# GpSimd issues three more transfers of an inverse transform, with a new order of work behind its last stage

## The chip, the cores and the metric

The kernel runs on one core of one Trainium2 chip. The metric is the device time of one execution in microseconds. Engines are named as the profile names them: PE (TensorE, matmuls), PEld (its weight loads), DVE (VectorE), ACT (ScalarE), POOL (GpSimd) and SP (SyncE, which only issues transfers). Transfers (DMAs) are issued from SP, ACT or POOL, and 16 DMA engines move the data.

## The reference

One layer on x of shape (2048 positions, 448 channels): a gated long convolution, then an MLP that mixes the positions. Cut to what matters:

```python
k_shift = sum_t k_pad[:, t:t+S, :] * shift_k[:, 3-t]         # short causal filter, 4 taps
kv = k_shift * v
y = irfft(rfft(kv, 2S) * rfft(ssm_k, 2S))[:S] + kv * ssm_D   # long convolution, per channel
h = x + layernorm(x) * y                                      # layernorm over the 448 channels
n = layernorm(h)
u = gelu(einsum("sd,sf->df", n, w1) + b1)                     # contracts the 2048 positions
out = h + (einsum("df,fs->ds", u, w2) + b2).T
```

All inputs are bfloat16; S = 2048, D = 448, F = 1792.

## The kernel before

Position s is split as s = 16 q + r, so a tile of row r has the 128 values of q on the partitions and the 448 channels in the free dimension. The transform of the convolution is done with matmuls in two stages. Between the stages data changes partitions, and that is done with SBUF-to-SBUF transfers.

**Forward stages.** k1 and u1 (first stages of the filter and of kv), k2 and u2 (second stages, `emit_stage2`, L1095 the matmuls).

**First inverse stage, i1** (`emit_products_i1`, L1151). It runs over eight pairs jj; pair jj holds the columns j = 2jj and 2jj + 1. For each half h (real and imaginary part) DVE forms products of the two spectra (L1161), PE multiplies by a constant table (L1178, 8 matmuls), and an evacuation copies the two PSUM banks to the tile TU (`evac`, L739 on ACT, L742 on DVE). Then transfers carry TU to TZ, the input of the second inverse stage, where the row r stands in the free dimension. For all pairs but the last, each column has two transfers (L1201): a large one of 112 partitions (196 KB), which fills rows 0 to 13 of TZ, and a small one of 16 partitions (28 KB), which fills rows 14 and 15. The large ones go over POOL, except for j = 3, which goes over SP; the small ones go over SP. The last pair, jj = 7, has four transfers of 98 KB instead (L1190), one for each column and half, which fill rows 2 to 15: three over SP and one over ACT. Rows 0 and 1 do not wait for them, since they take that pair's part from TU by extra matmuls (L1308).

**Second inverse stage, i2** (`emit_i2`, L1284). For each of the 16 rows r, PE does two matmuls with the transposed table ET (L1300; 4 more, L1308, for r = 0 and 1). Then a *gate* for r >= 4 (L1317 on ACT or L1319 on DVE: times the inverse deviation of x, plus 1), a *comb* on DVE (L1337 for r < 4, reading PSUM and the normalized x, called XN; L1327 otherwise), the statistics of h (L1343 and L1346 for r = 0 and 1; a square on ACT, L1355, and small POOL instructions L1365 to L1375 for the others), a power on POOL (L1379) and on DVE the normalized row Q (L1386).

**Beside it.** `emit_q` takes the statistics of x (DVE L1237 and L1239, POOL L1245 and L1248), `emit_xn` makes XN for r < 4 (POOL L1257, DVE L1260, ACT L1270), `emit_ct` transposes the table to ET in three late groups ct.0 to ct.2 (PE L1109, evacuated by ACT, L739), and `emit_warm` has 14 dummy matmuls (L1211) whose result is not used.

**MLP.** Seven column groups of the first product accumulate over the rows in seven of the eight PSUM banks (L1433), row by row as Q arrives, with the i2 matmuls of the later rows between them. Then come the other seven groups (L1443), the gelu (L1423) and the second product (L1455), whose rows are written out. The weights are loaded over SP: four loads of W1A (L1406), four of W1B (L1410) and four of W2 (L1417). All W1A loads but the first wait until the last pair's transfers have landed.

**What sets the order.** The table `ORDER` at the head of the file holds, for each engine, the list of its operations; each engine works through its list in order. An entry `step:n` or `step:a-b` names operations of a step. A planner (`schedule`, L323) walks through these lists only to place PSUM banks and to find which semaphore waits are needed; all waits come from data dependences. The entries that matter here:

- i1.1, i1.4, i1.6, i1.8, i1.10, i1.12, i1.14, i1.16 are the pairs jj = 0, 1, 2, 3, 4, 5, 6, 7. PE does them in the order 0, 6, 3, 4, 5, 2, 1, 7, so i1.4 (jj = 1) and i1.16 (jj = 7) are the last two.
- In such a step operations 9 and 18 are the evacuations of h = 0 and h = 1, and 19, 20, 21, 22 are the transfers: large and small of the even column, large and small of the odd one. In i1.4 the numbers are one lower (18 large of j = 2, 19 small of j = 2, 20 large of j = 3, 21 small of j = 3). In i1.16, 19 and 20 are the transfers of h = 0, and 21 and 22 those of h = 1.
- i2.1 and i2.2 are the matmuls of r = 0 and i2.3 its comb, i2.8 its Q; i2.9 and i2.10, i2.11, i2.16 the same of r = 1; i2.18 and i2.21 the combs of r = 2 and 3, i2.39 and i2.52 the Q of r = 4 and 6. q.n are statistics of x (q.2 for r = 2 and 3, q.3 and q.4 for r = 4 to 7, q.5 and q.6 for 8 to 11, q.7 and q.8 for 12 to 15), xn.n the steps of XN, mlp.r:n the matmuls of row r of the first product.

## Time and profile before

| what | value |
|---|---|
| runs | 173.05 us median of 3 (173.01 to 173.22) |
| profiled execution | 173.14 us, span 171.3 us, granted PE clock 1.000 |
| busy, share of the span | PE 94%, PEld 55%, DVE 59%, ACT 54%, POOL 34% |
| DMA | 35.15 MB, mean 205 GB/s |
| chain that ended last | PE 66%, ACT 17%, DMA 7%, DVE 5%, POOL 2% |
| first L1300 (i2) matmul | 75.27 us from the span's start |
| first L1433 (MLP) matmul | 81.08 us |

Times of day in the text are microseconds from the start of the span. A line of the chain of work that ended last gives start, length and what ran or was waited for. A line of the timeline gives start, length, engine, line, operation, tiles and, in brackets, how long the engine idled before and what released it; a q behind an engine's name means its sequencer, which issues transfers. A line of the waits gives who waited for whom, total, number of times and the longest. The data of most of the kernel lies in one tile called arena, and PSUM is called ps. The PE busy share counts pipelined matmuls, so it is read together with the chain.

### The profile page before, as it was taken

The numbers are of one execution on the slowest core, as the hardware profiler recorded it, in microseconds if no ns is written. First come the engines' busy times: TensorE is split into PE (matmuls) and PEld (weight loads), VectorE is DVE, ScalarE is ACT, GpSimd is POOL, SyncE is SP. The second block draws the span as 40 slices with busy tenths as digits, with TensorE's granted clock in tenths as the row PEclk, the third lists the DMA queues.
The fourth block names the chain that finished last, engine by engine and source line by source line (L and its number), as shares of the span: only waits on it lengthen the run. The fifth ranks groups of instructions, "written<-read, shape, count | busy, mean of one in ns | idle before, by whom it ended". The sixth has DMA issues, their size and how long they took to land.

```text
span 171.3 us, 3572 instructions
## 1 busy us (share of the span) xinstructions
PE 161.9 (94%) x1425; PEld 94.9 (55%) x1425; DVE 101.4 (59%) x188; ACT 92.6 (54%) x132; POOL 59.0 (34%) x151
## 2 busy tenths in 40 slices
PE   6999999789889999968999999999999999999994
PEld 2785755342334333544455555555567777777783
DVE  7998988859999999979989830000003123132231
ACT  3699698978999999979866537321210000000000
POOL 8346637571810686245897830000000000000000
PEclk9999999999999999999999999999999999999999
DMA  5999678593859757646899999990000111101111
GB/s 163 420 352 354 210 234 311 178 354 136 286 144 369 268 167 208 176 143 214 266 331 384 411 420 419 415 406 33 0 0 4 54 54 54 54 0 57 54 54 54
DMA packets 15652, 35.15 MB, mean 205 GB/s; under 512 B 3692, under 2 KB 9804, under 8 KB 15636
## 3 DMA queue, kind: packets, MB, share of 16 engines
q1 hardware_dynamic: 12588, 28.45, 45.6%
q0 software_dynamic: 2784, 6.29, 11.5%
q8 instruction: 11, 0.18, 0.4%
q10 hardware_dynamic: 264, 0.18, 0.3%
q14 instruction: 5, 0.04, 0.1%
HBM read 22.05 MB, written 1.84 MB: 139 GB/s over the span
## 4 chain that ended last, share of the span: by engine, by line
PE 66%; ACT 17%; DMA 7%; DVE 5%; POOL 2%; issue 1%; SPq 0%; DVEq 0%
PE ps L1455 25%; PE ps L1433 12%; PE ps L1443 12%; ACT arena L739 9%; DMA arena<-arena 7%; ACT arena L1070 4%; PE ps L1178 4%; PE ps L1095 3%; ACT arena L848 2%; PE ps L1026 2%; PE ps L1300 2%; POOL arena L1076 2%; PE ps L993 2%; DVE arena L1008 2%; PE ps L1060 1%; DVE arena L1337 1%
## 5 line engine op out<-in xcount | busy, mean ns | idle before, releaser
L1458 DVE SCALAR_TENSOR_TENSOR arena<-ps,arena 128x448 bf16<-128x448 f32 (+2 forms) x17 | 11.1, 656 | 56.9 <-PE ps L1455 56.9
L1455 PE MATMUL ps<-arena 128*128 128x448 bf16 (+2 forms) x238 | 42.7, 342 | 0.0
L1455 PEld LDWEIGHTS ps<-arena 128*128 128x128 bf16 x238 | 33.3, 145 | 9.5
L739 ACT CAST arena<-ps 128x896 bf16<-128x896 f32 x30 | 24.6, 1016 | 0.2 <-PE ps L1095 0.2
L1433 PE MATMUL ps<-arena 128*128 128x448 bf16 x112 | 22.5, 353 | 0.7 <-DVE arena L1375 0.7
L1070 ACT CAST arena<-ps 128x896 bf16<-128x896 f32 x24 | 20.5, 918 | 3.0 <-PE ps L1060 2.9
L1076 POOL DMA_DIRECT2D arena<-arena x32 | 17.5, 553 | 12.5 <-ACT arena L1070 10.4
L1443 PE MATMUL ps<-arena 128*128 128x448 bf16 x112 | 21.4, 352 | 0.0
L1423 ACT ACTIVATE arena<-ps,arena 128x448 bf16<-128x448 f32 x14 | 8.3, 634 | 18.9 <-PE ps L1443 14.7
L1095 PE MATMUL ps<-arena 128*64 128x448 bf16 x128 | 15.2, 359 | 2.6 <-DMA arena<-arena 1.0
L1433 PEld LDWEIGHTS ps<-arena 128*128 128x128 bf16 x112 | 10.8, 98 | 11.3 <-DVE arena L1375 1.1
L1161 DVE TENSOR_TENSOR arena<-arena 128x1792 bf16<-128x1792 bf16 x16 | 16.7, 1086 | 0.3 <-ACT arena L739 0.2
L1443 PEld LDWEIGHTS ps<-arena 128*128 128x128 bf16 x112 | 11.0, 98 | 10.2
L1060 PE MATMUL ps<-arena 128*32 128x448 bf16 x256 | 15.2, 355 | 0.8 <-DVE arena L1008 0.5
L1178 PE MATMUL ps<-arena 64*128 64x448 bf16 x128 | 14.5, 351 | 0.1
L1201 POOL DMA_DIRECT2D arena<-arena x13 | 7.7, 597 | 13.7 <-ACT arena L739 13.7
L1095 PEld LDWEIGHTS ps<-arena 128*64 128x64 f16 x128 | 5.8, 108 | 11.0 <-ACT arena L739 2.9
L1178 PEld LDWEIGHTS ps<-arena 64*128 64x128 f16 x128 | 6.1, 94 | 8.2 <-ACT arena L739 2.5
L1008 DVE TENSOR_TENSOR arena<-ps,arena 128x512 bf16<-128x512 f32 (+1 forms) x16 | 9.1, 619 | 2.1 <-PE ps L993 1.8
L739 ACT COPY arena<-ps 128x1024 bf16<-128x1024 bf16 (+1 forms) x8 | 7.8, 1022 | 4.5 <-PE ps L967 3.4
L1355 ACT ACTIVATE arena<-arena 128x448 bf16<-128x448 f32 x14 | 8.0, 573 | 4.0 <-DVE arena L1327 3.8
L1060 PEld LDWEIGHTS ps<-arena 128*32 128x32 f16 x256 | 5.1, 95 | 7.8 <-DVE arena L1008 2.5
(96 smaller groups left out, 195.1 us busy)
## 6 DMA issues: line engine op xcount, KB each, us to landing
arena<-in_B_w_dram SPq DMA_DIRECT2D x8, 896.0 KB, 6.5
arena<-in_B_w_dram SPq DMA_DIRECT2D x2, 2048.0 KB, 17.0
arena<-arena POOLq DMA_DIRECT2D x32, 112.0 KB, 3.3
arena<-arena SPq DMA_DIRECT2D x16, 224.0 KB, 3.2
arena<-in_B_w_dram SPq DMA_DIRECT2D x2, 1536.0 KB, 19.3
arena<-arena POOLq DMA_DIRECT2D x13, 196.0 KB, 4.3
arena<-in_A_k_dram SPq DMA_DIRECT2D x4, 448.0 KB, 5.3
arena<-in_A_v_dram SPq DMA_DIRECT2D x4, 448.0 KB, 8.4
```

The costliest lines, as they stand in the source:

```text
L739: return e.copy(out=dst(), in_=src())
L1008: return e.tensor_tensor(out=v, in0=u.rearrange("p t (r d) -> p t r d", d=64), in1=v, op=ALU.mult)
L1060: op("pe", lambda e, W, b=b, r=r, q=q, x=x, c0=c0: e.matmul(PS[32 * q:32 * q + 32, b.slots[x], 0:D], E[:, 2 * r + x, c0:c0 + 32], src[:, r ...
L1070: return e.copy(out=dst, in_=Ppair(b)) if W == "act" else e.tensor_copy(out=dst, in_=Ppair(b))
L1076: shuf[tag].append(op(q_, lambda e, W, g=g, i=i, a=a, nu=nu, jh=jh: e.dma_start(T[a + i:a + i + 4 * nu - 3:4].rearrange("p (j k) c d -> p ...
L1095: op("pe", lambda e, W, b=bs[h], h=h, j=j, c=c, par=par: e.matmul(PS[64 * par:64 * par + 64, b.slots[c], 0:D], FW[:, 64 * c:64 * c + 64], ...
L1161: op("dve", lambda e, W, m=m, i=i: e.tensor_tensor(out=MR(m.slots[0]).rearrange("p (x y) d -> p x y d", x=2), in0=TU[:, i].unsqueeze(2).br ...
L1178: k = op("pe", lambda e, W, b=bs[h], m=ms[h], par=par, t=t, tab=tab, xy=xy, P=P: e.matmul(Pb(b, par), tab[P, :], MR(m.slots[0])[P, xy, :], ...
L1433: op("pe", lambda e, W, r=r, fc=fc, b=bs[fc]: e.matmul(Pb(b), W1A[:, r, 128 * fc:128 * fc + 128], Q[:, r, :], start=(r == 0), stop=(r == R ...
L1443: op("pe", lambda e, W, r=r, fc=fc, b=b: e.matmul(Pb(b), W1B[:, r, 128 * (fc - n0):128 * (fc - n0) + 128], Q[:, r, :], start=(r == 0), sto ...
L1455: op("pe", lambda e, W, r=r, fc=fc, b=b, d0=d0, d1=d1: e.matmul(Pb(b)[:, d0:d1], W2[fc // 7][:, fc % 7, r:S:R], G[:, fc, d0:d1], start=(fc ...
L1458: op("dve", lambda e, W, r=r, b=b, A=A, d0=d0, d1=d1: e.scalar_tensor_tensor(out=X[:, r, d0:d1], in0=Pb(b)[:, d0:d1], scalar=bm[:, r:r + 1 ...
```

## The change

Three transfers change their issuer. The small transfers of the pair jj = 2 (i1.6:20 and i1.6:22) go from SP to POOL. One of the last pair's four (i1.16:21, h = 1 of column 14) goes from ACT to POOL.

```diff
-k = op("act" if h and par == 0 else "sp", lambda e, W, j=j, h=h, p0=p0: e.dma_start(
+k = op("pool" if h and par == 0 else "sp", lambda e, W, j=j, h=h, p0=p0: e.dma_start(
...
-for q_, a, b_, j0 in (("sp" if j == 3 else "pool", 0, 112, 0), ("sp", 112, 128, 14)):
+for q_, a, b_, j0 in (("sp" if j == 3 else "pool", 0, 112, 0), ("pool" if jj == 2 else "sp", 112, 128, 14)):
```

The lists in `ORDER` change from about the last two pairs of i1 on. On SP ten of the small transfers, which stood behind the last pair's and between the W1A loads, now stand ahead of i1.4:20, and two (i1.4:21 and :19) stand directly behind it; the W1A and W1B loads follow each other. On PE three more dummy matmuls stand ahead of i1.16, the table transposes come in another order, three dummies stand between the i2 matmuls, and the rows and the MLP's column groups come in another order. On DVE one small instruction of the statistics goes behind the first comb, and the combs of r = 2 and 3 go ahead of the statistics of r = 1. On ACT the gates of r = 4 to 6 go behind the squares of r = 2 and 3.

```diff
 PE
-warm.9 warm.11 warm.5 warm.8 warm.1 i1.16:1-7 i1.16:10-16 i1.16:8 i1.16:17 warm.10 warm.4 warm.7 warm.6 warm.0
-ct.2:0-7 warm.12 warm.3 ct.0:0-7 ct.1:0-6 warm.2 i2.1:0-1 i2.2:0-3 i2.9:0 ct.1:7 i2.9:1 i2.10:0-3 i2.28 i2.17
-i2.45 i2.20 i2.41 i2.32 i2.54 mlp.0:6 mlp.0:1 mlp.0:5 mlp.0:2-4 mlp.0:0 i2.58 mlp.1:6
+warm.9 warm.11 warm.5 warm.8 warm.1 warm.10 warm.0 warm.4 i1.16:1-7 i1.16:10-17 i1.16:8 ct.0:0-7 warm.2 ct.1:0-2
+warm.6 ct.2:0-6 ct.1:3-7 i2.1:0-1 i2.2:0-3 ct.2:7 i2.9:0-1 warm.7 i2.10:0-3 i2.17 i2.45 i2.20 i2.32 warm.3
+warm.12 i2.41 i2.28 i2.54 mlp.0:4 mlp.0:2 mlp.0:1 mlp.0:5 mlp.0:0 mlp.0:6 i2.58 mlp.0:3 mlp.1:4
 ACT
-i1.16:18 i1.16:9 i1.16:21 ct.2:8 ct.0:8 xn.4 ct.1:8 xn.5 i2.29 i2.46 i2.19 i2.33 i2.22 i2.42 i2.31
+i1.16:18 i1.16:9 ct.0:8 xn.4 ct.1:8 ct.2:8 xn.5 i2.46 i2.19 i2.22 i2.29 i2.42 i2.33 i2.31
 DVE
-q.4:0 q.4:2-3 q.4:1 q.3:1-3 q.5:0 q.5:2-3 q.5:1 q.6:2 q.6:0-1 q.7:0 q.7:2 xn.3:1 i2.3 q.6:3 i2.4 i2.11 i2.5
-i2.12 i2.6 i2.18 i2.21 q.7:3 i2.13 i2.8 i2.14 i2.55 i2.30 i2.16 q.7:1
+q.3:1-2 q.4:0 q.3:3 q.4:2 q.5:0 q.5:2 q.5:1 q.4:3 q.4:1 xn.3:1 q.5:3 q.6:2 q.6:0 q.7:2 q.7:0 i2.3 q.6:1 q.6:3 i2.4
+i2.11 i2.5 i2.18 i2.6 i2.21 i2.12 i2.13 i2.8 i2.14 i2.55 i2.30 i2.16
 POOL
-i1.6:19 i1.6:21 i1.4:18 q.4:4-5 q.2:4-5 xn.3:0 q.6:4-5 ... i2.49:1-2 q.8:4 i2.50 q.8:5 i2.51
+i1.6:19 i1.6:21 i1.6:20 q.2:4 i1.4:18 i1.6:22 q.2:5 xn.3:0 i1.16:21 q.4:4-5 q.6:4-5 ... i2.49:1-2 q.8:4-5 i2.50 i2.51
 SP
-i1.6:22 i1.1:20 i1.1:22 i1.4:20 i1.16:22 i1.16:20 i1.16:19 w1a.1 i1.12:22 i1.14:20 i1.4:21 i1.4:19 w1a.2 i1.6:20
-i1.14:22 i1.10:20 i1.10:22 w1a.3 i1.8:22 i1.12:20 i1.8:20 w1b
+i1.14:20 i1.1:20 i1.1:22 i1.12:22 i1.10:22 i1.10:20 i1.12:20 i1.8:20 i1.8:22 i1.14:22 i1.4:20-21 i1.4:19
+i1.16:22 i1.16:20 i1.16:19 w1a.1 w1a.2 w1a.3 w1b
```

66 rows, old and new, of the table ORDER are left out of this document.

## The prediction

> **What bounds the kernel now.** I read the page's chain first, then the chain in order of time, then the waits, then the issues around the place where the chain leaves the engines. The chain, cut to the stretch that the change touches and to what follows:
>
> ```profile
> 69.06 1.13 ACT arena L739
> 70.20 0.28 issue
> 70.48 4.74 DMA arena<-arena
> 75.22 0.05 issue
> 75.27 0.55 PE ps L1300 x2
> 75.82 0.77 PE ps L1308 x4
> 76.59 0.02 issue
> 76.62 0.68 DVE arena L1337
> ...
> 80.63 0.40 DVE arena L1386
> 81.02 0.07 DVE arena L1375
> 81.10 1.48 PE ps L1433 x7
> ...
> 105.16 21.19 PE ps L1443 x112
> 126.34 42.08 PE ps L1455 x231
> ```
>
> Columns are start, length and what (us). From 81.08 (first L1433) to 168.42 the chain is PE alone, back to back, and the change adds and drops no matmul there. So the time is the start of the first L1433 matmul plus a constant, unless PE stalls later. Before it stand one transfer of 4.74, 1.3 of PE work for row r = 0, and a DVE chain of 4.4 that ends with Q of r = 0 (L1386). The waits (total, times, longest) say the same:
>
> ```profile
> PE ps L1300 <- DMA arena<-arena: 1.3, 1, 1.3
> DVE arena L1337 <- PE ps L1308: 0.9, 1, 0.9
> PE ps L1433 <- DVE arena L1375: 0.7, 1, 0.7
> ```
>
> The transfer is i1.4:18, the last large one of GpSimd. Around it the issues are:
>
> ```profile
> 66.97 3.92 SPq L1201 DMA_DIRECT2D arena<-arena  x4
> 67.24 1.17 POOL L1201 DMA_DIRECT2D arena<-arena  x2 [1.48 <-ACT arena L739]
> 70.48 0.59 POOL L1201 DMA_DIRECT2D arena<-arena  x1 [2.08 <-ACT arena L739]
> 72.26 2.19 SPq L1190 DMA_DIRECT2D arena<-arena  x3
> ```
>
> The fourth of SP's is i1.4:20, the other large half of the same pair, issued at 70.21. The answer on line L1201 gives the landings of GpSimd's transfers:
>
> ```profile
> DMA to landing us min/median/max: 3.0/4.3/5.4
> ```
>
> Why does i1.4:18 take 4.74 and not 3.0? I added up the trace's DMA packet records (of 500 bytes and more) in quarter microseconds. When GpSimd alone moves one transfer, 8.0 packets are in flight (58.25, 63.25, 64.50); where two of its successive transfers overlap there are 13 to 14 (66.00, 67.50). So one uses 8 of 16 engines and the next the other 8. But from 72.25 to 74.25 GpSimd's and SP's packets sum to 8 again (1.0+7.6, 4.1+4.0, 6.1+1.8, 6.1+2.0, 6.9+1.2, 6.0+2.2, 4.9+3.2, 2.9+5.5): i1.4:18 and i1.4:20 share one set of 8 while the other lies idle. The first data packet of i1.4:18 leaves 1.94 after its issue, against 1.17 for i1.14:19. They land at 75.22 and 75.06.
>
> **The change, part by part.** Times are of the profiled execution: 173.14, its span 171.3 and 1.8 around it; the three runs have a median of 173.05, 0.09 lower.
>
> *The small transfers on GpSimd.* i1.6:20 goes in at 68.41, right behind i1.6:21, into the 2.08 that POOL idles there (0.59 by the L1201 rows), and q.2:4 (0.2 to 0.5) after it still ends before 70.2: i1.4:18 is issued at 70.48 as before. It is one more transfer in GpSimd's sequence, so i1.4:18, until now the 13th, becomes the 14th and takes the other set. Alone there it should need what i1.14:19 and i1.10:19 needed alone (2.98 and 2.97): landing 73.46; i1.6:21, ahead of it on that set, had all but one packet moved by 72.0, so I take 73.5 to 74.0. The ends of this cost are no gain (75.22, still shared) and 73.46; I take the lower since the packet sums are its nearest row. The Trainium skill, page "DMA: Bandwidth & Descriptors", section "Why a DMA increments its semaphore by 16 and not by 1", says that a transfer from SP takes the lowest-numbered engines, and one of GpSimd's the next ones behind a round-robin cursor; the trace agrees (the sums of 8 and 13 to 14), but no run here shows the cursor moved by a small transfer. i1.4:20 has its set to itself: first packet 71.54 as before, 130 KB/us as it moved in 71.5 to 72.5, 200 KB: 73.1, landed 73.3.
>
> *i1.6:22 and i1.16:21 on GpSimd.* i1.6:22 costs POOL 0.59 from 71.07 (idle before: 1.04). q.2:5 and xn.3:0 (0.71 and 0.19) follow and end at 72.7, nearly 2 earlier than before. i1.16:21 waits for the evacuation i1.16:18 and holds back q.4:4-5 (0.24 + 1.05), which ends at 75.0 and not 73.5; its readers are the gates of r = 4 to 7 on ACT, first at 77.4. ACT loses an issue of 1.51, which left it idle 0.78; the L739 work behind it then waits for PE anyway (0.37 idle before ct.1:8), so I count 0.
>
> *SP.* Eleven transfers of 28 KB leave the stretch 77.56 to 86.33 behind the last pair: ten go to earlier places on SP, one (i1.6:20) to POOL, and i1.6:22 leaves 66.97. Each costs SP 0.67. i1.14:20, i1.1:20 and i1.1:22 fit at 60.1 to 62.1, where SP idles; i1.12:22 waits for its evacuation (ACT ends it at 63.71) and with six more takes 7 x 0.69 = 4.9: 68.6, ahead of i1.4:20 at 70.2. i1.4:21 and :19 then fill 70.9 to 72.3. On SP's engine set the seven are 2 packets per engine each, some 0.2 (their landings after w1a.1 are 0.2 apart): 1.4 in 65 to 70, and GpSimd's three transfers on that set, 1.4 each (first to last packet of i1.14:19), fill 4.2 of the 6.8 from 64.5 to 71.3. What doesn't fit into the rest could push i1.4:20 by up to 0.5; I take 0, and 0.5 would still land it by 73.8. The W1A loads move from 77.1, 80.4 and 83.8 to some 76.4 to 77.8; L1433 needs the second only at 87.97 (landed 82.07 before): 0.
>
> *Dummy matmuls.* Eight (L1211) instead of five now stand before i1.16: 3 x 0.19 = 0.58 later. The evacuations i1.16:18 and :9 end at 72.77 and 73.57, SP issues at 72.80, 73.60 and 74.31. With i1.4:20's tail gone, the last one's packets start 1.33 after issue (as i1.4:20's did), take 12 x 41 ns and land near 76.3; before it was 77.12. i1.16:21 from POOL, issued near 73.05, lands at 76.0 with the lone 2.97. Behind i1.16 PE has 2 dummies and 23 transposes (1.7) and reaches i2.1 at 73.4, before the landing. The three dummies put into the row matmuls (0.57) lie in PE's wait for Q (0.66 now).
>
> *DVE.* This becomes the bound. From 69.80 to 75.69 it works without a break; the new order has the same nine L1237 and the same small ones less one L1239 (0.1), so i2.3 (L1337, r = 0) cannot start before 75.55. xn.3:1 is reached at 73.0, its POOL input is ready at 72.7. PE gives r = 0 at 73.75 + 1.35 = 75.1. So i2.3 starts at 75.55 in place of 76.62: 1.07 earlier. If the transfer lands after 74.2, the landing decides again. Behind i2.3 the new order holds the same instructions up to Q of r = 0 (one comb of r = 0, 1, 2, 3 each, two L1343, four small ones, var, Q): 4.46, L1433 at 80.0. Rows 2 and 3 come in time: landing 76.3, PE results 76.9 and 77.6, XN from ACT by 77.5; DVE wants them at 77.6 and 78.3.
>
> *What is late next.* ACT now does the gates of r = 4, 6, 5 behind both squares (L1355). The second square needs the comb of r = 3 (78.9) and takes 0.57 + 0.19: 79.8. Three gates of 0.6 to 0.7 behind it end at 81.65, that is 1.65 after the first L1433, against 0.1 (r = 5) and 1.27 (the last gate, r = 6) now. Its bank is needed by mlp.0:3 at +1.52, its value by DVE at +1.63 for a Q that PE wants with only 0.05 to spare at mlp.2: 0.1 to 0.4 of new stall. q.8:4-5 now waits for two L1239 behind i2.39, some 0.35 later, about the slack of Q of r = 6 (0.4): 0. I take 0.25 in all.
>
> Sum: -1.07 + 0.25 = -0.82; 173.14 - 0.82 = 172.32, against the median 172.2.
>
> **Rivals.** (a) *Nothing is freed.* The set does not change, or i1.4:20 is pushed as much as i1.4:18 gains. For it: all rows show large transfers in strict turns, none after a small one. Landing 75.2, DVE no earlier: 173.05, up to 173.3 with ACT's late gates. The Trainium skill speaks for this rival: the same page, section "Issuing engines are not separate DMA queues", says that transfers of all issuers end up on the same 16 engines and that issuing from more of them saves only the time of the issue. By that rule the time stays at 173.05. The packet sums speak against it, since half the engines were idle.
>
> (b) *Slower: the last pair comes late from GpSimd.* Every row r >= 2 needs all four L1190 transfers. If i1.16:21 takes what i1.6:21 took (5.43) and not 2.97, it lands at 78.5; 7 rows and 2 dummies then take 16 x 0.19 = 3.05 and the first L1433 starts at 81.6, 0.5 late: 173.55. It decides from a landing at 78.0 on, that is 4.95 after issue; two of 13 transfers took longer (5.08 and 5.43), both with twice the bytes and queued behind others. Against it: by 73 nothing large is left ahead of it.
>
> (c) *The gain is eaten.* The transfers are early, but gates, banks or the push of i1.4:20 cost 0.8 and more: 172.8 to 173.2.
>
> **Numbers.** Forecast 0.70, alone between 171.95 (the DVE bound with no stall) and 172.65 (0.4 of stall and 0.3 of late landing). Rival (a) 0.11, (b) 0.09, (c) 0.10. About 0.2% (0.35) is what can be told from no change. Faster: the forecast and a little of (c), 0.72; same: most of (a) and (c), 0.15; slower: (b) and the tail of (a), 0.13. The range reaches from the DVE bound over (a) and (c): 171.9 to 173.2; only (b) and tails lie outside.
>
> **What would show it.** Right: the first L1300 near 73.7, the chain's transfer near 3 long, no idle time before the first L1337 (75.55), the first L1433 near 80.0, the last pair landed by 76.4. Wrong: i1.4:18 still lands near 75 and its packets still sum to 8 with SP's (a); L1300 waits a second time on DMA past 78 (b); L1433 stalls on L1386 or on ACT between 80 and 86 (c). A granted clock below 1.00 would also break the sum; it was 1.00 in every stretch.

## The result, and the profile after

| | before | after |
|---|---|---|
| median of 14 runs, us | 173.2 | 174.82 |
| ratio, 95% interval | | 1.0063 [1.0041, 1.0085] |
| profiled execution, span | 173.14, 171.3 | 173.91, 171.9 |

The change makes the kernel 0.6% slower; the forecast was 172.2 us and faster. Executions at a granted clock of 0.99 are 1 to 2% longer, and the ratios leave them out but for a few (three of after2's twelve, one each of e_bank's and e_bq's, two of before's): without these, the means of after2, e_bank and e_bq stand at 1.0056, 1.0024 and 1.0025 of before's.

The chain of work in order of time, after, from the evacuation of i1.4 to row 6 of the MLP (start, length, what):

```profile
70.55 4.30 DMA arena<-arena
74.85 0.09 issue
74.94 0.54 PE ps L1300 x2
75.47 0.76 PE ps L1308 x4
...
76.85 0.77 PE ps L1308 x4
77.62 0.02 issue
77.65 0.70 DVE arena L1337
78.34 0.05 issue
78.39 0.95 PE ps L1300 x4
79.34 0.02 issue
79.36 0.69 DVE arena L1337 x2
...
88.28 1.15 POOL arena L1248
89.43 0.08 issue
89.51 0.28 POOL arena L1375
89.79 0.07 issue
89.87 1.04 POOL arena L1379
90.90 0.03 issue
90.93 0.53 DVE arena L1386
91.46 0.05 issue
91.51 0.55 PE ps L1433 x2
```

Three things are to be seen. The transfer i1.4:18 (issued at 70.55) takes 4.30, against 4.74 before and 2.97 in the forecast. Then the chain, which before stayed on DVE from the comb of r = 0 to Q, leaves DVE at 78.34 for four L1300 matmuls on PE and comes back: the comb of r = 1 (77.65) holds back PE's matmuls of r = 7 and r = 3, and r = 3 holds back DVE, which idles 0.30 there. In before the combs of r = 1, 2 and 3 follow on DVE with no PE between them (the x4 are two combs, each with a read of its sum):

```profile
77.96 0.58 DVE arena L1337
...
79.26 1.21 DVE arena L1337 x4
```

Last, before, PE ran without a wait from the first L1433 on; now L1433 waits at 91.51 for a Q that hangs on POOL's L1248 (q.8:5). The waits of after (total, times, longest):

```profile
PE ps L1300 <- DMA arena<-arena: 1.5, 1, 1.5
DVE arena L1337 <- PE ps L1308: 1.1, 1, 1.1
PEld ps L1300 <- DVE arena L1337: 0.8, 1, 0.8
PE ps L1300 <- DVE arena L1337: 0.4, 1, 0.4
```

DVE still idles 1.1 ahead of the comb of r = 0, where the forecast had none. The fourth line is new: PE waiting for a comb. The issues that answer to those shown of before, in the timeline:

```profile
60.25 12.14 SPq L1201 DMA_DIRECT2D arena<-arena  x13
67.31 1.70 POOL L1201 DMA_DIRECT2D arena<-arena  x3 [1.48 <-ACT arena L739]
70.55 1.18 POOL L1201 DMA_DIRECT2D arena<-arena  x2 [0.52 <-ACT arena L739]
72.65 2.20 SPq L1190 DMA_DIRECT2D arena<-arena  x3
```

SP issues 13 transfers from 60.25 on without another kind between them; POOL's three at 67.31 are i1.6:19, i1.6:21 and the small i1.6:20, its two at 70.55 i1.4:18 and the small i1.6:22.

Stage by stage, from the trace of each kernel, in us. The columns i1.6:19 and i1.4:18 are the time from issue to landing of two large GpSimd transfers whose issuer no kernel here changes. The next column runs from the dummy warm.9, which stands behind i1.4 on PE, so that what went before drops out; the last two start where the one before them ends. The two profiles marked * are of executions at a mean granted clock of 0.99; it was below 1.00 only between 10 and 20 us (0.71 to 0.95 in stretches of 5 us) and 1.00 in every stretch behind, so these columns, which all lie later, can be compared:

| kernel | ratio, 95% interval | i1.6:19 | i1.4:18 | warm.9 to first L1300 | to first L1433 | to first L1455 |
|---|---|---|---|---|---|---|
| before | | 4.62 | 4.74 | 6.99 | 5.81 | 45.10 |
| before2 | 1.0017 [0.9991, 1.0044] | 4.64 | 4.74 | 7.25 | 5.80 | 45.10 |
| after | 1.0063 [1.0041, 1.0085] | 5.29 | 4.30 | 6.59 | 6.33 | 45.44 |
| after2 | 1.0084 [1.0050, 1.0117] | 5.20 | 4.25 | 7.12 | 6.34 | 45.44 |
| e_flip | 0.9986 [0.9965, 1.0008] | 4.94 | 4.16 | 6.45 | 5.80 | 45.10 |
| e_sp | 1.0046 [1.0014, 1.0078] | 5.07 | 4.13 | 7.43 | 5.80 | 45.18 |
| e_tr | 1.0035 [1.0008, 1.0063] | 5.95 | 4.31 | 6.60 | 5.80 | 45.79 |
| e_ord | 0.9991 [0.9964, 1.0018] | 4.37 | 3.99 | 6.24 | 5.95 | 45.46 |
| e_q8 | 1.0054 [1.0028, 1.0080] | 5.44 | 4.41 | 6.71 | 6.39 | 45.30 |
| e_bank | 1.0030 [0.9996, 1.0063] | 5.89 | 4.05 | 6.34 | 5.94 | 45.37 |
| e_fix2 | 1.0013 [0.9988, 1.0038] | 4.19 | 3.95 | 6.25 | 5.94 | 45.37 |
| e_fix3* | 0.9977 [0.9945, 1.0008] | 4.07 | 3.72 | 6.02 | 6.01 | 45.30 |
| e_bq | 1.0035 [1.0005, 1.0064] | 5.55 | 4.57 | 6.86 | 6.03 | 45.30 |
| e_spa | 1.0036 [1.0009, 1.0063] | 4.98 | 4.13 | 6.56 | 5.80 | 45.10 |
| e_sp7 | 1.0009 [0.9976, 1.0042] | 5.91 | 4.70 | 6.95 | 5.81 | 45.10 |
| e_sp3 | 0.9960 [0.9935, 0.9984] | 4.33 | 4.32 | 6.57 | 5.81 | 45.09 |
| e_late | 1.0010 [0.9978, 1.0043] | 4.31 | 4.25 | 6.59 | 5.80 | 45.35 |
| e_sp21 | 0.9989 [0.9958, 1.0020] | 5.64 | 3.76 | 6.05 | 5.80 | 46.46 |
| e_best* | 0.9975 [0.9957, 0.9994] | 5.02 | 3.94 | 6.53 | 5.81 | 45.10 |
| e_best_b | 0.9959 [0.9924, 0.9994] | 5.86 | 4.07 | 6.54 | 5.81 | 45.10 |

From the first L1455 to the end it is 45.13 to 45.20 in all of them. So in the profiles of before and after, the first L1300 gains 0.40 from warm.9 on (0.33 from the span's start), the next stretch loses 0.52 and the MLP 0.34. The last two columns repeat to 0.02 between profiles of one kernel; the transfers do not (after and after2: 6.59 and 7.12), and there the ratios, most of them of nine to twelve runs, weigh more than one profile.

### The profile page after: what moved, and what is told of

It is laid out like the page before. It is cut to its first block, busy times and chain, and to the rows that moved or that the text cites. A ratio compares the mean times of both kernels' runs of the same rounds, so it can differ in the third digit from the quotient of the medians.

```text
span 171.9 us, 3570 instructions
## 1 busy us (share of the span) xinstructions
PE 162.7 (95%) x1425; PEld 95.4 (56%) x1425; DVE 100.6 (59%) x187; ACT 93.0 (54%) x133; POOL 61.0 (35%) x154
## 3 DMA queue, kind: packets, MB, share of 16 engines
q1 hardware_dynamic: 12540, 28.39, 45.1%
q0 software_dynamic: 2912, 6.45, 11.9%
## 4 chain that ended last, share of the span: by engine, by line
PE 64%; ACT 17%; DMA 7%; DVE 6%; POOL 2%; issue 1%; SPq 0%; DVEq 0%
PE ps L1455 24%; PE ps L1443 12%; ACT arena L739 8%; PE ps L1433 8%; DMA arena<-arena 7%; ACT arena L1070 5%; PE ps L1095 5%; PE ps L1178 4%; ACT arena L848 2%; PE ps L1060 2%; PE ps L1026 2%; PE ps L967 2%; ACT arena L740 2%; PE ps L1300 2%; DVE arena L1386 2%; PE ps L993 1%
## 5 line engine op out<-in xcount | busy, mean ns | idle before, releaser
L1455 PE MATMUL ps<-arena 128*128 128x448 bf16 (+2 forms) x238 | 42.7, 342 | 0.0
L1455 PEld LDWEIGHTS ps<-arena 128*128 128x128 bf16 x238 | 33.3, 145 | 9.5
L1433 PE MATMUL ps<-arena 128*128 128x448 bf16 x112 | 22.7, 353 | 0.2
L1076 POOL DMA_DIRECT2D arena<-arena x32 | 17.6, 553 | 12.0 <-ACT arena L1070 10.4
L1443 PE MATMUL ps<-arena 128*128 128x448 bf16 x112 | 21.5, 353 | 0.0
L1433 PEld LDWEIGHTS ps<-arena 128*128 128x128 bf16 x112 | 10.7, 98 | 11.1 <-ACT arena L1317 0.6
L1201 POOL DMA_DIRECT2D arena<-arena x15 | 8.8, 593 | 12.2 <-ACT arena L739 12.2
L1300 PE MATMUL ps<-arena 128*128 128x448 bf16 x32 | 8.0, 353 | 1.9 <-DMA arena<-arena 1.5
L1317 ACT ACTIVATE arena<-ps,arena 128x448 f32<-128x448 f32 x10 | 7.0, 720 | 4.7 <-PE ps L1300 4.7
```

Of the source, the lines that this page charges most:

```text
L1076: shuf[tag].append(op(q_, lambda e, W, g=g, i=i, a=a, nu=nu, jh=jh: e.dma_start(T[a + i:a + i + 4 * nu - 3:4].rearrange("p (j k) c d -> p ...
L1300: k = op("pe", lambda e, W, b=b, r=r, h=h: e.matmul(Pb(b), ET[:, 2 * r + h, :], TZ[:, r, h, :], start=(h == 0), stop=(h == 1 and r >= NZ)) ...
L1433: op("pe", lambda e, W, r=r, fc=fc, b=bs[fc]: e.matmul(Pb(b), W1A[:, r, 128 * fc:128 * fc + 128], Q[:, r, :], start=(r == 0), stop=(r == R ...
L1443: op("pe", lambda e, W, r=r, fc=fc, b=b: e.matmul(Pb(b), W1B[:, r, 128 * (fc - n0):128 * (fc - n0) + 128], Q[:, r, :], start=(r == 0), sto ...
L1455: op("pe", lambda e, W, r=r, fc=fc, b=b, d0=d0, d1=d1: e.matmul(Pb(b)[:, d0:d1], W2[fc // 7][:, fc % 7, r:S:R], G[:, fc, d0:d1], start=(fc ...
```

## The experiments

### The two kernels again

after2 is the changed kernel, unchanged.

> The changed kernel unchanged, profiled a second time, because its profiled execution (173.91) was 0.8 over that of before while the runs' medians lie 1.1 to 1.6 apart. Two theories on the change are in play. Queue: the last large transfer of GpSimd (i1.4:18) was held by GpSimd's own backlog (i1.6:21 ahead of it had moved its data by 71.9 in both profiles), so the other engine set gained only 0.4; the loss comes later, mostly where the statistics q.8 now stand ahead of i2.50 on POOL (PE waits 0.3 at mlp.6). Small: the other engine set would gain about 1.5, but SP's small transfers, moved into 60 to 70, push the large ones. Queue expects here again the landing of i1.4:18 at 74.6 to 75.0, the first L1433 at 81.1 to 81.4 and a wait of 0.3 at mlp.6; Small expects the landing to follow the small ones, 74.8 or later. If a run is a full 1 us slower than the first profile, this profile shows where.

Measured: 1.0084 [1.0050, 1.0117] (the mean named above is 1.0056). The two stretches behind the first L1300 repeat (6.34 and 45.44), the transfers don't: i1.4:20 landed at 75.26 here and set the first L1300, 74.13 in the first profile, where i1.4:18 (74.85) set it. i1.4:18 landed at 74.63, within Queue's bounds; the first L1433 (81.65) did not come within them.

before2 is the kernel before, unchanged.

> The kernel before, unchanged, for a second profile. Theory Spread: the 4.74 of i1.4:18 that the prediction took from the one profile of before is a draw from a spread, as 3.99 and 4.12 in two experiments in which its engines were not changed say; it expects i1.4:18 at 4.0 to 4.6 from issue to landing and the first L1300 6.2 to 6.8 after warm.9. Rival Fixed: the same order gives the same transfers, 4.6 to 4.9 and 6.9 to 7.1. Ratio 1.000 by both.

Measured: 1.0017 [0.9991, 1.0044], i1.4:18 again 4.74 and the first L1300 7.25 after warm.9. Spread fell: the 4.74 was not a lucky draw. But 33 of the 35 runs of before beside it go from 172.43 to 174.56, so a difference of 0.2% between two kernels needs more than the three runs (173.01 to 173.22) from which the 0.2% of the forecast was taken.

### The parts of the change, one at a time

e_flip takes from the change only a small transfer on GpSimd ahead of i1.4:18:

```diff
-for q_, a, b_, j0 in (("sp" if j == 3 else "pool", 0, 112, 0), ("sp", 112, 128, 14)):
+for q_, a, b_, j0 in (("sp" if j == 3 else "pool", 0, 112, 0), ("pool" if j == 5 else "sp", 112, 128, 14)):
 POOL
-... i1.6:19 i1.6:21 i1.4:18 ...
+... i1.6:19 i1.6:21 i1.6:22 i1.4:18 ...
 SP
-... i1.6:22 i1.1:20 i1.1:22 i1.4:20 ...
+... i1.1:20 i1.1:22 i1.4:20 ...
```

> The kernel before with one small transfer (i1.6:22) moved from SP to POOL, right behind i1.6:21, and nothing else; so i1.4:18 takes the engine set that i1.4:20 does not use, and SP's other small transfers stay behind the last pair. Queue: i1.4:18 lands at 74.3 to 74.8 (it still starts near 72), the first comb (L1337) starts 0.4 to 0.8 earlier, time 172.4 to 172.9 beside 173.2 of before. Small: nothing pushes now, i1.4:18 lands at 73.5 to 74.0, the first comb starts at 75.7, time 172.1 to 172.4.

Measured: 0.9986 [0.9965, 1.0008]. The engine set did change: GpSimd's and SP's data packets in flight sum to 14.2 in 72.5 to 73.0, against 8.0 in before in the same half microsecond (8.1 in before2; 14.2 in after). The landing hardly did: 74.76, 4.16 after issue. Small falls, since the flip alone should have gained 1.5; of Queue the landing and the comb came true (76.18 for 76.62), the time did not (median 173.21, for 172.4 to 172.9). And the edit does more than the expectation says: i1.1:20 and i1.1:22, which waited behind i1.6:22 on SP (67.70 and 68.41 in before), are now issued at 60.35 and 61.07. e_fix2 and e_fix3 below have the same side effect.

e_sp takes only SP's list (with i1.6:22 and i1.6:20 on SP too, ahead of i1.4:20):

```diff
 SP
-... i1.6:22 i1.1:20 i1.1:22 i1.4:20 i1.16:22 i1.16:20 i1.16:19 w1a.1 ... w1a.2 ... w1a.3 ...
+... i1.14:20 i1.1:20 i1.1:22 i1.12:22 i1.10:22 i1.10:20 i1.12:20 i1.8:20 i1.8:22 i1.14:22 i1.6:22 i1.6:20
+i1.4:20-21 i1.4:19 i1.16:22 i1.16:20 i1.16:19 w1a.1 w1a.2 w1a.3 ...
```

> The kernel before with SP's list alone changed: the ten small transfers stand ahead of the last two pairs as in the changed kernel (i1.6:22 and i1.6:20 directly ahead of i1.4:20, still on SP), the loads follow each other; all other lists and all issuers stay. Queue: the small ones cost the large ones little, i1.4:18 lands at 75.2 to 75.6, time 173.1 to 173.5. Small: it lands at 76 or later, time 173.8 to 174.3.

Measured: 1.0046 [1.0014, 1.0078], from only four of twelve executions; first L1300 7.43 after warm.9. Small's time came true, but neither theory's landing: i1.4:18 landed at 74.15. What the first L1300 waited for is i1.4:20, at 75.17: with i1.6:22 and i1.6:20 directly ahead of it, SP issued it 2.77 after warm.9, in every other kernel here 1.93 to 2.08. So e_sp shows that this list costs, but part of its cost is the issue, which the changed kernel does not delay.

e_q8 puts the order around q.8 back in the changed kernel:

```diff
 DVE
-... i2.21 ... i2.16 i2.34 ... i2.39 q.7:1 q.7:3 i2.69 ...
+... i2.21 q.7:3 ... i2.16 q.7:1 i2.34 ... i2.39 i2.69 ...
 POOL
-... q.8:4-5 i2.50 i2.51 ...
+... q.8:4 i2.50 q.8:5 i2.51 ...
```

> The changed kernel with the places of q.7:1, q.7:3 (DVE) and of i2.50 between q.8:4 and q.8:5 (POOL) as before the change; all else as changed. Queue: PE's wait of 0.3 at mlp.6 (L1433 on L1386) goes, the time is 0.3 to 0.4 under the changed kernel's, still above before. Small: no difference in front of the MLP, at most 0.3 behind it; the rest of the loss stays in front of the MLP.

Measured: 1.0054 [1.0028, 1.0080]. From the first L1433 to the first L1455 it takes 45.30 in place of 45.44: 0.14 of the 0.34, less than the 0.3 to 0.4 of Queue. PE's wait ahead of the first L1433 of row 6 falls from 0.125 to 0.052.

e_tr is the changed kernel (issuers, SP's list, POOL's list up to i2) with the lists of before for PE, DVE and ACT and for POOL's tail.

```diff
 PE, DVE
-the lists of after
+the lists of before
 ACT
-... i1.16:18 i1.16:9 ct.0:8 ...
+... i1.16:18 i1.16:9 ct.2:8 ...
 POOL
-... q.8:4-5 i2.50 ...
+... q.8:4 i2.50 q.8:5 ...
```

> The transfers of the change alone: its issuers, its SP list and its POOL list up to i2, with the orders of PE, DVE and ACT and the tail of POOL as before. Theory Two halves: issuers and SP list come to nothing (the flip -0.5 at the first L1300, SP's early small transfers +0.4), and the loss of the change lies in the orders of PE, DVE and ACT. It expects the first L1300 6.6 to 7.1 after warm.9 (before 6.99), first L1300 to first L1433 5.8 as before, first L1433 to first L1455 45.1, and a ratio of 0.997 to 1.001. Rival Transfers: what costs 0.5 behind the first L1300 is the late last pair or the early work on POOL; it expects 6.2 or more from the first L1300 to the first L1433, and a ratio above 1.003.

Measured: 1.0035 [1.0008, 1.0063]; 5.80 to the first L1433 as before, so the transfers don't cost there. But the MLP took 45.79: in this mixture, which neither kernel has, DVE comes to a Q (i2.16, r = 1) before POOL is done, and PE waits. The waits of e_tr:

```profile
PE ps L1300 <- DMA arena<-arena: 0.9, 1, 0.9
PE ps L1433 <- DVE arena L1375: 0.7, 1, 0.7
PE ps L1433 <- DVE arena L1386: 0.5, 1, 0.5
```

The third line is that stall (a step of 0.85 between two matmuls instead of 0.19). It alone is about the 0.35% of the ratio, so this run doesn't show that the transfers cost anything.

e_ord is the reverse: the issuers and the SP list of before with the lists of after for PE, DVE and ACT and for POOL's tail; i1.16:21 is on ACT again.

```diff
 PE, DVE
-the lists of before
+the lists of after
 ACT
-... i1.16:18 i1.16:9 i1.16:21 ct.2:8 ct.0:8 ...
+... i1.16:18 i1.16:9 i1.16:21 ct.0:8 xn.4 ...
 POOL
-... i1.6:19 i1.6:21 i1.4:18 q.4:4-5 q.2:4-5 ...
+... i1.6:19 i1.6:21 q.2:4 i1.4:18 q.2:5 xn.3:0 q.4:4-5 ...
```

> The orders of the change alone: its lists for PE, DVE and ACT and its tail of POOL, with the issuers and the SP list of before (i1.16:21 on ACT again, the two small ones on SP). The banks of PSUM come out otherwise than in the change: r = 7 gets the bank of the dummy warm.7 and r = 3 that of ct.2, so neither waits for a comb. Theory Bank: the 0.5 of the change between the first L1300 and the first L1433 is the wait of r = 7 for the bank of r = 1; without it 5.8 to 6.0, then 45.3 to 45.4 to the first L1455, ratio 1.001 to 1.004. Rival Order: the sequence of the instructions itself (r = 3 behind r = 7, dummies among the rows) costs it, whatever the bank: 6.2 to 6.4, ratio 1.004 to 1.007.

Measured: 0.9991 [0.9964, 1.0018], and 5.95 to the first L1433, not 6.33. The same instructions in the same order take 0.38 less, because the planner puts r = 7 into another bank here. Bank stands for this stretch, Order falls. Bank's ratio (1.001 to 1.004) did not come, since the first L1300 was 0.75 earlier than in before (6.24 after warm.9). The MLP keeps its loss (45.46).

### The bank of r = 7

In the changed kernel the planner gives r = 7 (i2.45) the PSUM bank of r = 1, which the comb of r = 1 frees at 78.34. r = 3 (i2.20) stands behind r = 7 on PE and would have had a free bank. e_bank moves one dummy of the changed kernel and with it all later banks by one place:

```diff
 PE
-... warm.1 warm.10 warm.0 warm.4 i1.16:1-7 ... ct.1:3-7 i2.1 ...
+... warm.1 warm.10 warm.4 i1.16:1-7 ... ct.1:3-7 warm.0 i2.1 ...
```

> The changed kernel with one dummy (warm.0) moved from ahead of i1.16 to just ahead of i2.1, where PE idles: r = 7 then gets a bank that ACT's evacuation i1.16:18 freed and r = 3 another of these, in place of the bank of r = 1. Theory Bank: PE's wait of 0.4 ahead of r = 7 is gone, the comb of r = 3 follows without idle time, and from the first L1337 to the first L1433 it is 4.5 to 4.7 in place of 4.99; ratio to before 1.002 to 1.005, 0.3 to 0.5 us faster than the changed kernel. Rival Order: 4.9 to 5.1 as in the changed kernel, ratio 1.005 to 1.009.

Measured: 5.94 to the first L1433, and 4.61 of it from the first L1337 (4.99 in after). The waits of e_bank:

```profile
PE ps L1300 <- DMA arena<-arena: 1.3, 1, 1.3
DVE arena L1337 <- PE ps L1308: 0.9, 1, 0.9
PEld ps L1211 <- DVE arena L1337: 0.4, 1, 0.4
```

No L1300 waits for a comb any more. It is the dummy warm.3 (L1211) whose weight load does, and behind it PE waits for Q of r = 0 anyway. Ratio 1.0030 [0.9996, 1.0063] against 1.0063 and 1.0084: the trace shows 0.39 us gone, 0.22% of the time; the ratios alone would not settle it.

### With the causes put right, one after the other

e_fix2 is e_bank with SP's list as before (i1.6:20, i1.6:22 and i1.16:21 stay on POOL):

```diff
 SP
-... i1.14:20 i1.1:20 i1.1:22 i1.12:22 ... i1.14:22 i1.4:20-21 i1.4:19 i1.16:22 ... w1a.1 w1a.2 w1a.3
+... i1.1:20 i1.1:22 i1.4:20 i1.16:22 ... w1a.1 i1.12:22 i1.14:20 i1.4:21 i1.4:19 w1a.2 i1.14:22 ... w1a.3 ...
```

> The changed kernel without the two causes found: SP's list as before (the two small ones of the change stay on GpSimd, i1.16:21 too) and the dummy warm.0 ahead of i2.1, so that r = 7 doesn't wait for the bank of r = 1. If the parts add up (the flip -0.1%, SP's list +0.5%, the orders 0, the bank +0.3 to +0.5%), the ratio is 0.997 to 1.001 and first L1300 to first L1433 takes 5.9 to 6.0. If something else of the change costs (the last pair from GpSimd, GpSimd's extra issues), it stays at 1.003 or above.

Measured: 1.0013 [0.9988, 1.0038], the first L1300 6.25 after warm.9, then 5.94. The ratio lies between the two expectations, the stage times are as the sum of the parts has them.

e_fix3 has the order around q.8 of e_q8 as well:

```diff
 DVE, POOL
-... i2.39 q.7:1 q.7:3 ... | ... q.8:4-5 i2.50 ...
+... i2.21 q.7:3 ... i2.16 q.7:1 ... | ... q.8:4 i2.50 q.8:5 ...
```

> The changed kernel without all three causes found: SP's list as before, the dummy warm.0 ahead of i2.1 (bank of r = 7), and q.7:1, q.7:3 and i2.50 in the order of before (Q of r = 6). Theory Three causes: first L1433 to first L1455 falls from 45.37 to 45.1 to 45.25, and the ratio is 0.997 to 1.000. Rival Rest: another 0.2 us or more of the change stays, ratio 1.001 to 1.003.

Measured: 0.9977 [0.9945, 1.0008], and 45.30 from the first L1433 to the first L1455, a little over the 45.1 to 45.25 of Three causes. Rival Rest falls by its ratio.

e_bq is e_fix3 with the SP list of the change: bank and q.8 put right, nothing else.

```diff
 SP
-... i1.1:20 i1.1:22 i1.4:20 i1.16:22 ... (the list of before)
+... i1.14:20 i1.1:20 i1.1:22 i1.12:22 ... i1.14:22 i1.4:20-21 i1.4:19 i1.16:22 ... (the list of after)
```

> The changed kernel with its own SP list, and the bank of r = 7 and the order around q.8 put right (the version with all three put right was at 0.9977). Theory Three causes: SP's list costs 0.2 to 0.5% here too: ratio 1.000 to 1.003, first L1300 to first L1433 5.9 to 6.0, first L1433 to first L1455 45.2 to 45.3. Rival: beside the mended orders SP's list costs nothing, ratio 0.997 to 0.999.

Measured: 1.0035 [1.0005, 1.0064]; 6.86, 6.03, 45.30. Against e_fix3 that is +0.58%, some 1.0 us (0.8 us with the mean of e_bq named above), and the intervals just overlap. The stage times say where: 6.86 for 6.02 up to the first L1300, and no difference of more than 0.02 behind it. SP's list is what remains of the loss; the rival falls.

### SP's small transfers

e_spa is the kernel before with ten of them early and i1.4:21 and :19 late:

```diff
 SP
-... i1.6:22 i1.1:20 i1.1:22 i1.4:20 i1.16:22 i1.16:20 i1.16:19 w1a.1 ...
+... i1.14:20 i1.1:20 i1.1:22 i1.12:22 i1.10:22 i1.10:20 i1.12:20 i1.8:20 i1.8:22 i1.14:22 i1.4:20 i1.16:22
+i1.16:20 i1.16:19 w1a.1 i1.4:21 i1.4:19 w1a.2 i1.6:22 i1.6:20 w1a.3 ...
```

> The kernel before with ten of SP's small transfers moved ahead of i1.4:20, as the change has them, while i1.4:21 and i1.4:19 stay behind the last pair (i1.6:22 goes there too, since its place is taken). Theory Push: the packets of the ten stand in the queues of SP's engines ahead of i1.4:20 and beside GpSimd's large transfers; the first L1300 comes 0.3 to 0.8 later on the average, ratio 1.003 to 1.006. Rival Last pair: what costs is i1.4:21 and i1.4:19 between i1.4:20 and i1.16:22, so that without them nothing is lost: ratio 0.998 to 1.001.

Measured: 1.0036 [1.0009, 1.0063]. Rival Last pair falls: the loss is there without i1.4:21 and :19 ahead of the last pair. Its profiled execution (172.35) was the shortest of its executions, so its 6.56 is not typical.

e_sp7 has only the last seven of the ten early, e_sp3 only the first three:

```diff
 SP (e_sp7)
-... ct0.1:2-4 i1.6:22 i1.1:20 i1.1:22 i1.4:20 ...
+... ct0.1:2-4 i1.12:22 i1.10:22 i1.10:20 i1.12:20 i1.8:20 i1.8:22 i1.14:22 i1.4:20 ...
 SP (e_sp3)
-... ct0.1:2-4 i1.6:22 i1.1:20 i1.1:22 i1.4:20 ...
+... ct0.1:2-4 i1.14:20 i1.1:20 i1.1:22 i1.6:22 i1.4:20 ...
```

> The kernel before with only seven of SP's small transfers (i1.12:22 to i1.14:22) ahead of i1.4:20, those that the change issues at 63.4 to 69; i1.14:20, i1.1:20 and i1.1:22, which the change issues at 60 to 62, go behind the last pair. Theory Push: it is these seven, whose packets run beside GpSimd's last large transfers, that cost; ratio 1.002 to 1.005. Rival Early: it is the three at 60 to 62, beside the ct0.1 transfers; ratio 0.998 to 1.001.

Measured: 1.0009 [0.9976, 1.0042], which decides nothing between the two.

> The kernel before with only i1.14:20, i1.1:20 and i1.1:22 issued at 60 to 62, where SP idles, and the other seven behind the last pair as before. Theory Early: these three, beside the ct0.1 transfers and GpSimd's large ones, are what ten early small transfers cost: ratio 1.002 to 1.005. Theory Sum: no single few of them cost it; three are under what can be told: ratio 0.999 to 1.001.

Measured: 0.9960 [0.9935, 0.9984], faster. Early falls clearly: the three at 60 to 62, where SP idles, cost nothing and gain some 0.4%. (Both theories had priced them at zero or worse.) What the ten cost must then come from the seven or from all ten together.

What the seven do is seen in a transfer that all these kernels issue alike: i1.6:19, GpSimd's large one, issued at 66.8 to 67.7 (near 70 in the two profiles marked *). The answer on line L1201 for that one instruction, first of e_fix2 (SP's list as before), then of e_bq (SP's list as after):

```profile
L1201 POOL DMA_DIRECT2D arena<-arena x1: 587/587/587, 67.4 to 67.4; - x1
DMA to landing us min/median/max: 4.2/4.2/4.2
```

```profile
L1201 POOL DMA_DIRECT2D arena<-arena x1: 590/590/590, 67.7 to 67.7; - x1
DMA to landing us min/median/max: 5.6/5.6/5.6
```

The third column of the table has it for all: with the seven early it is 4.98 to 5.95 in nine profiles of nine; without them, and with no further large transfer on SP, 4.07 to 4.94 in eight of eight. So the seven delay GpSimd's large transfer, by 1.0 in the mean (5.48 against 4.43). And every kernel with all ten early has a ratio of 1.003 or more (eight of eight; 1.0024 or more with the means named above; though three of them have the bank's wait as well and e_tr its own stall), every other one 1.0017 or less (eleven of eleven). But the first is not what makes the second: e_sp7 has i1.6:19 at 5.91 and a ratio of 1.0009, and e_best_b, with i1.6:21 on SP, has 5.86 and 0.9959.

What the list costs is seen nearer to the first L1300, in the two transfers that it waits for, and only between kernels that have i1.4:18 on other engines than i1.4:20 by a small transfer. SP's landings are read from the semaphore records of the traces, and times are again from issue to landing. From e_fix2 to e_bank and from e_fix3 to e_bq nothing but SP's list changes: i1.4:20 goes from 3.20 to 4.15 and from 3.22 to 4.35, i1.4:18 from 3.95 to 4.05 and from 3.72 to 4.57, the first L1300 from 6.25 to 6.34 and from 6.02 to 6.86. With e_flip, after, after2, e_tr and e_q8 beside them, i1.4:20 takes 3.20 to 3.62 with SP's list as before (three profiles) and 3.85 to 5.00 with the changed list (six), which has ten of them ahead of i1.4:20 and two right behind. So the list delays the last pair of large transfers; how much of that reaches the first L1300 scatters from 0.1 to 0.8 in the two pairs.

### What holds i1.4:18

e_sp21 takes one large transfer off GpSimd in the kernel before:

```diff
-("sp" if j == 3 else "pool", 0, 112, 0)
+("sp" if j in (3, 5) else "pool", 0, 112, 0)
 POOL
-... i1.6:19 i1.6:21 i1.4:18 ...
+... i1.6:19 i1.4:18 ...
 SP
-... i1.6:22 i1.1:20 i1.1:22 i1.4:20 ... w1a.2 i1.6:20 ...
+... i1.6:21 i1.1:20 i1.1:22 i1.4:20 ... w1a.2 i1.6:22 i1.6:20 ...
```

> The kernel before with the large transfer i1.6:21 issued by SP in place of GpSimd, in the place of the small i1.6:22, which goes behind the last pair on SP. One large transfer less stands ahead of i1.4:18 on GpSimd, and i1.4:18 moves to the other set of engines as well. Theory Backlog: i1.4:18 was late because GpSimd's own transfers were still being worked off when it was issued; with one less it lands at 73.4 to 74.2, and i1.4:20, behind i1.6:21 on SP's engines, by 74.3; the first L1337 is then set by DVE near 75.7 to 75.9 and the first L1433 at 80.2 to 80.5 (before 81.08), ratio 0.995 to 0.998. Rival Rate: what limits is the sum of all bytes on the engines, not GpSimd's own sequence: the later of the two lands at 74.6 or after, first L1433 80.6 or later, ratio 0.998 to 1.001.

Measured: i1.4:18 in 3.76, near the shortest of the table (landed 74.37, 0.2 later than Backlog's bound), first L1300 6.05 after warm.9, no idle time of DVE ahead of the first L1337 (at 75.79), first L1433 at 80.26. The rest is as Backlog has it; and then the gain is lost, 0.9989 [0.9958, 1.0020]. The chain of e_sp21:

```profile
86.23 6.35 DMA arena<-arena
92.67 0.35 PE ps L1300
```

i1.8:20, the last small transfer in SP's list and one place later than before, landed at 92.58 and PE waited 1.05 for it: the other end of the same list.

e_best mends that (and issues i1.1:20 and :22 early):

```diff
 SP
-... ct0.1:2-4 i1.6:22 i1.1:20 i1.1:22 i1.4:20 i1.16:22 ...
+... ct0.1:2-4 i1.1:20 i1.1:22 i1.6:21 i1.4:20 i1.6:22 i1.16:22 ...
```

> The kernel before with the large transfer i1.6:21 on SP, with i1.6:22 right behind i1.4:20 on SP (in the experiment ahead it stood at the end and its row waited for it) and the small i1.1:20 and i1.1:22 where SP idles near 60. Theory Backlog: i1.4:18 lands 3.7 to 3.9 after issue and DVE sets the first L1337 (no idle time ahead of it); first L1433 at 80.0 to 80.5, 45.1 to the first L1455, time 0.5 to 0.9 below before, ratio 0.995 to 0.997. Rival: the transfers on SP's engines now hold i1.4:20 (landing past 74.8), ratio 0.998 to 1.002.

Measured: 0.9975 [0.9957, 0.9994], faster than both kernels. e_best_b is the same kernel. (That every stage was longer in the first profile, as the next expectation says, is wrong: from warm.9 on the stages of the two profiles are the same to 0.01; what the first lost lies ahead of warm.9, at 70.99 there and at 68.72 here.)

> The version with i1.6:21 on SP again, unchanged, for a profile at the full granted clock (0.99 in its first, in which every stage is longer). Theory Backlog: i1.4:18 lands at most 4.1 after issue, DVE has at most 0.3 of idle time ahead of the first L1337, first L1433 at 80.1 to 80.6; ratio 0.995 to 0.999. Rival: the landing still decides, 0.5 or more of idle time there.

Measured: 0.9959 [0.9924, 0.9994]. i1.4:18 takes 4.07, but i1.4:20, behind i1.6:21 on SP, lands at 75.22 and sets the first L1300. The waits of e_best_b:

```profile
PE ps L1300 <- DMA arena<-arena: 0.9, 1, 0.9
DVE arena L1337 <- PE ps L1308: 0.5, 1, 0.5
```

Half of each theory, then: DVE's idle time is down from 0.9 to 0.5, not to 0.3. And as e_sp3, with two of the same early transfers and no change of i1.6:21, is as fast, and i1.4:18 takes 3.72 to 3.99 in e_fix3, e_fix2 and e_ord too, where nothing was taken off GpSimd ahead of it, the gain can't be put down to the backlog.

e_late asks why the first L1300 came early in e_ord as well, where no transfer was changed. It moves three dummies:

```diff
 PE
-... warm.1 i1.16:1-7 ... i1.16:17 warm.10 warm.4 warm.7 warm.6 warm.0 ct.2:0-7 ...
+... warm.1 warm.10 warm.4 warm.0 i1.16:1-7 ... i1.16:17 warm.7 warm.6 ct.2:0-7 ...
```

> The kernel before with three dummies (warm.10, warm.4, warm.0) moved from behind i1.16 to ahead of it, as many as the change has there: i1.16 and its evacuations come 0.5 to 0.6 later, and so do the four transfers of the last pair, and nothing else changes. It asks why the first L1300 came 0.5 to 0.6 earlier in the experiment with the orders alone, in which no transfer was changed. Theory Room: the last pair's packets then no longer run beside i1.4:20 and i1.4:18 on the same engines, which land 0.4 to 0.6 earlier; first L1300 at most 6.5 after warm.9 (before 6.99 and 7.24), ratio 0.996 to 0.999. Rival Draw: the landing of one profile is a draw; 6.8 to 7.3, ratio 0.999 to 1.002.

Measured: first L1300 6.59 after warm.9, between the two theories, and 1.0010 [0.9978, 1.0043]; 0.25 of the MLP's 45.35 is a row (i2.93) that waits for a small transfer behind the last pair, which now lands later. Not settled.

## Why the prediction was wrong

**The transfer, the first failing step.** "Alone there it should need what i1.14:19 and i1.10:19 needed alone (2.98 and 2.97)". The set changed as the step said, and the small transfer changed it: the sums of packets are 14.2, 13.9 and 11.5 in the three half microseconds from 72.5, where before had 8. That part of the mechanism is shown. The Trainium skill, page "DMA: Bandwidth & Descriptors", section "Why a DMA increments its semaphore by 16 and not by 1", has a GpSimd transfer on fewer than 16 engines take the next ones from a round-robin cursor; these sums agree with it for a small transfer too. The size was wrong: i1.4:18 took 4.30 and 4.25, not 2.97. In the profiles of the table it took 3.72 to 4.74, on either set; no run reached 2.97. The row at 2.98 came out of an idle GpSimd, and the one at 2.97 had two large transfers ahead of it that landed within 1.7 of its issue. i1.4:18 has i1.6:21 and the small i1.6:20 ahead of it, which landed 3.2 and 3.3 after its issue (73.72 and 73.89). Among the profiles in which it has the idle set by a small transfer, it took 3.72 and 3.95 where the one ahead landed 2.1 to 2.2 after its issue (e_fix3, e_fix2) and 4.05 to 4.57 where that was 2.9 to 3.4. That is a correlation; e_sp21 and e_best_b, with one large transfer less ahead (3.76 and 4.07), do not show the backlog as the cause. The rows 5.08 and 5.43, which the prediction names in its rival (b), were the warning that a lone row is not typical, and it used them only for i1.16:21. By the ratio, the idle set is worth 0.14% (e_flip, an interval that holds zero, and with two small transfers early as well); the step's 1.07 is 0.6%.

On this point another section of that page of the Trainium skill, "Issuing engines are not separate DMA queues", came nearer than the step: it has all issuers share the same 16 engines, so that another issuer saves only the time of the issue. The packets show that half the engines were idle before the change; the time says that it hardly mattered.

**SP's list, "I take 0".** The prediction bounded the push by 0.5 on i1.4:20 and looked for it there. The place was right and the size was not. Against before it doesn't show (i1.4:20 lands 3.85 and 5.00 after issue in after and after2, 4.85 and 5.22 in before's two profiles), since there the shared engines hold it. Against kernels in which it has its engines to itself it does: 3.20 to 3.62 without the changed list (the forecast's 73.3 is 3.1 after issue), 3.85 to 5.00 with it, 0.95 more in the mean. GpSimd's transfers are pushed too: i1.4:18 by 0.4 in the mean of the same profiles, i1.6:19 by 1.0. That is the second condition of rival (a): i1.4:20 is pushed by about what i1.4:18 gains (4.74 to 3.94 in the mean without the list). The price is 0.2 to 0.6% by the ratios (e_bank against e_fix2 +0.17%, e_spa +0.36, e_bq against e_fix3 +0.58), that is 0.3 to 1.0 us. The prediction added up SP's packets and GpSimd's in 64.5 to 71.3, found them to fit (1.4 and 4.2 of 6.8), and took what fits to cost nothing. Why what fits still costs, no run shows. This and the step above left little of the gain of 1.07: 0.33 in the profile of after.

**DVE as the bound.** Not reached, since the landing came first (idle 1.11). But e_sp21, with the DVE list of before, bears the step out: where the transfer was early enough, DVE had no idle time and i2.3 started at 75.79, against the 75.55 forecast for the new order.

**"Behind i2.3 ... the same instructions ...: 4.46", "rows 2 and 3 come in time".** Row 2 did (its comb at 78.34, before 79.18). Row 3 did not (DVE idled 0.30 ahead of its comb at 79.36), and not for the reason checked. The prediction asked when its transfers land (76.3 forecast, 77.30 measured) and when PE is free, but not which PSUM bank each row gets in the new order, and who has to read that bank first. r = 7 got the bank of r = 1, r = 3 stood behind r = 7: 4.99. e_bank, e_fix2 and e_ord, with the same order of rows and other banks, have 4.60 and 4.61; the remaining 0.14 is the order's own. "Banks" were a word in rival (c), without a price.

**Late gates 0.25, q.8 0.** Their sum is near the 0.34 measured, the shares are not. The gates' stall at mlp.0:3 is 0.09 (a step of 0.28 instead of 0.19). The other stall is a step of 0.48 ahead of row 6, 0.29 more than usual. q.8:5 itself ends as before (89.43, before 89.37). But i2.50, which in before went in ahead of it (87.44), now stands behind it (89.51), so that POOL's power i2.51 starts at 89.87 in place of 89.33 and Q of r = 6 (i2.52) at 90.93 in place of 90.08. The prediction counted q.8:4's wait for DVE, not that i2.50 changes its place on POOL. With the old order around q.8 the stall is 0.22, and the MLP 0.14 shorter in e_q8, though the stretch ahead of it is 0.06 longer.

**What held.** No rival (b): i1.16:21 from GpSimd landed at 76.19, for 76.0 forecast. W1A's earlier loads cost PE nothing: no matmul of the MLP waits for a transfer in after. i1.4:18 was issued at 70.55, as before.

**In sum**: what the profile of after shows is -0.33 for the landing (forecast -1.07), +0.52 for the bank and the order of rows (0), +0.34 in the MLP (+0.25): +0.53 of the span's 0.56. The ratios have it at 1.0 to 1.1 us (1.0056 taken for after2), more than the profile: its first L1300, 6.59 after warm.9, is among the earlier ones of the kernels with SP's early list (up to 7.43). With SP's list, the bank and q.8 put back, the rest of the change is at 0.9977 [0.9945, 1.0008]: some of the forecast gain may be there, 0.4 us of the 1.07, in an interval that holds zero. But e_fix3 issues i1.1:20 and i1.1:22 early too, and e_sp3, with these two, one more and no change of issuer, is at 0.9960; so the gain can't be put down to the idle engines.

Open is why i1.4:18 needs 3.7 and more on idle engines, what makes the landing of i1.4's transfers vary by half a microsecond where neither their issuers nor their sets differ (e_ord, e_late, e_sp3 against before), and how the seven small transfers and the three share the blame and the gain: the ratios of e_sp7 (1.0009) and e_sp3 (0.9960) don't add up to that of e_spa (1.0036).

## What to carry to other kernels

For the time that a transfer will need, take the row with the same work ahead of it and beside it, not the shortest row: on idle engines i1.4:18 took 3.7 to 4.6, where the shortest rows had 2.97. When the order of PE's work changes, list for each matmul which bank it takes and which reader frees that bank, before calling a row in time: one dummy more or less shifts them all. Small transfers moved into an issuer's idle time can gain or cost: here three at 60 to 62 gained 0.4%, ten up to 69 lost as much. And check what else moves when one entry leaves an in-order list: in e_flip two transfers behind it went out 7 us earlier.

## What the runs showed of the hardware

A small GpSimd transfer moves the next large one to other engines than SP's large transfer has: 8 packets in flight without it, 14 with it (before, e_flip). Seven transfers of 28 KB from SP lengthen a 196 KB transfer of GpSimd beside them from 4.1 to 4.9 us to 5.0 to 6.0 us, though their bytes sum to no more than one such transfer. SP's own large transfer, alone on its engines, goes from 3.2 to 3.6 us to 3.9 to 5.0 us when ten such small ones go out ahead of it and two right behind. And a stage of the engines repeats to 0.02 us between executions, while the landing of the same transfer moves by more than 1 us (i1.4:20 in the changed kernel: 3.85 and 5.00 from issue).
